# Attention with token mixing on one core: one batch instead of two mixed by seven products, single accumulator banks, and transfers issued by ScalarE

## The chip, the cores and the metric

The kernel runs on one core of one Trainium2 chip. The metric is device microseconds of one execution, from start to end. Three runs of the kernel before were timed; one further execution was recorded by the profiler, and every number of the profile is from that one.

## The reference, cut to what matters

Four batches, eight heads, 768 tokens, head size 64. The attention is masked: a query sees a key only when both fall to the same one of 16 cluster centroids. Its output is the input x (4 x 768 x 512) of a second part, the token mixing, and the change is in that part:

```python
    theta = x @ w_theta
    cos_t, sin_t = (np.cos(theta), np.sin(theta))
    zr = x * cos_t
    zi = x * sin_t
    yr = np.einsum('ts,bsd->btd', w_tok_r, zr)
    yi = np.einsum('ts,bsd->btd', w_tok_i, zi)
    y = yr + yi
    u = x + y
    return (u + np.maximum(u @ w_ch, 0.0)).astype(np.float32)
```

`w_tok_r` and `w_tok_i` are 768 x 768, `w_theta` and `w_ch` 512 x 512. All is float32 to the eye of the caller.

## The kernel before, in words

**The parts.** The attention of all batches runs first and leaves x transposed in device memory (`xT_d`). The mixing then goes batch by batch, b = 0 to 3, and in each batch over six tiles of 128 tokens. The tiles are numbered through, n = 6b + t. Matmuls are taken as three products of high and low parts (`hi`, `lo`; the names with h and l at the end), so each float32 product is three matmuls.

**One tile's angle.** `theta_parts` splits the tile's columns of x (`xs`, one DMA on SP's queue, line 925) into `xh` (a cast on ScalarE, line 935) and `xl`. `rotation_angle` makes theta in one PSUM bank `tp` by 12 matmuls 128x512 (line 659). `rotation_reduce` takes it modulo 2 pi on VectorE (`kk`, `rab`, lines 666 to 668), and ScalarE takes the absolute value (line 670) and sine and cosine (line 985 in plain batches, 964 in the others). `rotation_turn` transposes the tile's own block `xb` into `xn` (VectorE, line 652) and then issues the loads of the next tile's block: `xb` has one buffer, and four DMAs of 64 KB fill it (line 647, on SP's queue). VectorE multiplies sine and cosine by `xn` (lines 987 and 971).

**The plain way of mixing** (`mix`, batches 0 and 1, as `PLAIN = 2` says). Each tile adds into y, one PSUM tile of six banks [128, 6, 512], with 48 matmuls (line 1024), 288 in a batch. Then `channel_plain` comes: `add_y` adds y to x (twelve VectorE instructions, line 1152; casts `uh` on ScalarE, line 1154; low parts `ul` on GpSimd, line 1155), `channel_products` multiplies by `w_ch` in eight groups of 12 matmuls (line 1162; the banks are two single ones `cp` and the six of y), and `channel_out` takes the maximum with zero, adds and writes `ot` (VectorE, line 1169, two buffers), which a DMA on SP's queue carries out (line 1171).

**The way by seven products** (`mix_forms`, batches 2 and 3). The two 768 x 768 weights are cut in quarters and summed into seven "forms" per tile (`W_SUM`, `make_forms`: VectorE sums `sum` line 1061, ScalarE casts 1062, GpSimd low parts 1063, DMAs out to device memory as `wf` 1064; the sources are loaded into `ws` tiles). `load_forms` brings a tile's forms back, seven DMAs on SP's queue. `split_z` makes the matching sums of z (`zt` on VectorE, lines 1087 to 1090; `zf` on ScalarE and GpSimd, 1096 and 1097). Each half of the channels then needs 126 matmuls 128x384 over six tiles (line 1112), 252 in a batch. Product 4 has the bank `four`, the other six have the banks of y. Between the halves, `add_products` adds the seven sums to x (VectorE, line 1121) and frees the banks. The second half of z is kept in device memory (`zd`, stored on line 977, loaded back as `zb` on line 1077). `split_u_part` and `channel` are what `add_y` and `channel_plain` are in the plain way.

**The order.** Attention and plain batches are ordered by a list scheduler with its own model of each engine; it may move instructions far from where the program has them. The part by seven products keeps the order in which it is written (`in_order(begin)`). There, tile n + 2 has its angle while tile n is mixed. The making of the forms is a generator (`new_forms`) that the loop over plain tiles advances, five steps at each tile from n = 1 on:

```python
        mix(b, t)
        if 0 < n < PLAIN * NT - 1:
            for _ in range(5):
                next(new_forms, None)
        if n == PLAIN * NT - 2:
            run(new_forms)
            load_forms(0)
            load_forms(1)
```

**Queues and semaphores.** All DMAs of the mixing are issued by SP in the kernel before. Each DMA, whoever issues it, reports on one of eight completion semaphores taken in turn (`DMAHW0` to `DMAHW7` in the lists below), and waits until the DMA that used the same semaphore before it is done.

Of the kernel before, what the change touches and what calls it, by code (L numbers as in the profile page):

```python
# [9 lines left out]
F32 = mybir.dt.float32  # L10
# [4 lines left out]
ALU = mybir.AluOpType  # L15
AX = mybir.AxisListType
PSUM = bass.MemoryType.PSUM
# [24 lines left out]
def kernel(  # L42
# [595 lines left out]
    def load_blocks(n):  # L638
        if n == B * NT:
            return  # L640
        b, t = divmod(n, NT)
        xb = blocks[n] = ma[0].tile([P, DM], F32, tag="xb", name=f"xb{n}")


        for a in range(P // 32):
            src = xT_d[b][:, :, t * P + 32 * a:t * P + 32 * a + 32]
            nc.sync.dma_start(  # L647
                out=xb[32 * a:32 * a + 32].rearrange("c (n m r) -> c n m r", n=NP, m=P // 32),
                in_=src.rearrange("(m c) n r -> c n m r", c=32))

# [194 lines left out]
    def mpool(name, bufs=1, **kw):  # L845
        return mctx.enter_context(tc.tile_pool(name=name, bufs=bufs, **kw))

    pm = [mpool("pm0", space=PSUM)]
    y = mpool("py", space=PSUM).tile([P, 6, 512], F32, name="y")
    pm.append(mpool("pm1", space=PSUM))  # L850
    mx = mpool("mx")
    ma.append(mpool("ma1"))
# [12 lines left out]
    def mbank(name):  # L865
        banks[0] += 1
        return pm[(banks[0] - 1) % 2].tile([P, 512], F32, tag="bank", name=name)
# [51 lines left out]
    def load_columns(n):  # L919

        b, t = divmod(n, NT)
        if 0 < b < B:
            columns[n] = mxs.tile([P, NCT, P], F32, tag="xs", name=f"xs{n}")
            with tc.issue_after(last_load[0].ins):
                nc.sync.dma_start(out=columns[n], in_=xT_d[b][:, :, t * P:(t + 1) * P])

    PLAIN = 2
    turning = {}

    def theta_parts(n, eng, after=None):  # L930
# [43 lines left out]
    def keep_turned(b, t, rab):  # L974
        zs[b, t] = rab
        z_d[b, t] = dram.tile([P, 2, DM // 2], F32, tag=f"z{t}", name=f"zd{b}_{t}", bufs=2)
        nc.sync.dma_start(out=z_d[b, t], in_=rab[:, :, DM // 2:DM])

    def rotate(b, t, rab, xn):
        if b < PLAIN:  # L980
# [21 lines left out]

    def y_at(d, c0, c1):
        bank, c = divmod(d * S + c0, 512)
        return y[:, bank, c:c + c1 - c0]

    def cuts(d, c0=0, c1=S):

# [55 lines left out]
                nc.sync.dma_start(out=w_f[t][:, m - 1], in_=f(to))  # L1064
                yield

    def load_forms(t):
        for m in ORDER:
            nc.sync.dma_start(out=f(forms[t][m]), in_=w_f[t][:, m - 1])

    second = {}
# [28 lines left out]
    four = {}  # L1100

    def product(m):
        return four[0][:, 0:HS] if m == 4 else y[:, Y_AT[m], 0:HS]

    def mix_forms(tiles, first, last):

# [9 lines left out]
    def add_products(b, h, k):  # L1116

        x = xts[b][:, 2 * h:2 * h + 2].rearrange("p d (l n) -> p (d l) n", l=2)

        def add(to, of, op):  # L1120
            nc.vector.tensor_tensor(out=to, in0=to, in1=of, op=op)  # L1121

        def twice(m):
            return product(m).unsqueeze(1).broadcast_to([P, 2, HS])

        if k == 0:
            add(x[:, 0:3:2], twice(4), ALU.add)
            add(x[:, 1:4:2], twice(3), ALU.subtract)
            add(x[:, 0:4:3], twice(1), ALU.add)
        else:  # L1130
            add(x[:, 0:4:3], y[:, 2:4, 0:HS], ALU.subtract)
            add(x[:, 1:3], y[:, 2:4, 0:HS], ALU.add)
            add(x[:, 3], product(6), ALU.add)
            add(x[:, 0], product(7), ALU.subtract)

    def split_u_part(b, h, us, eng):

# [35 lines left out]
    def channel_plain(b):  # L1173
        us = [add_y(b, ch * HS, (ch + 1) * HS) for ch in range(2)]
        for x in range(2 * NCT):
            ch, e = divmod(x, NCT)
            cp = (mbank(f"cp{b}_{x}") if x < 2 else y[:, x - 2])[:, 0:HS]
            channel_products(cp, e, us[ch], range(NCT))
            channel_out(b, e, ch, cp)

# [19 lines left out]
    for n in range(PLAIN * NT):  # L1200
        b, t = divmod(n, NT)
        theta(*divmod(n + AHEAD, NT))
        if b == 0:
            weights_after[0] = splits[n + 1]
            next(late_weights, None)
        mix(b, t)
        if 0 < n < PLAIN * NT - 1:
            for _ in range(5):
                next(new_forms, None)
        if n == PLAIN * NT - 2:  # L1210
            run(new_forms)
            load_forms(0)
            load_forms(1)
        if t == NT - 1:
            if b == PLAIN - 1:
                load_forms(2)
                load_forms(3)
            channel_plain(b)
            load_x(b + 1)
# [22 lines left out]
        if n in turning:  # L1242
            turned(n)

    load_forms(4)
    before(PLAIN * NT + 2)
    z = split_z(PLAIN, 0, 0)
    for b in range(PLAIN, B):
        for t in range(NT - 1):
            n = b * NT + t  # L1250
            done(n + 1)
            angle(n + 2)
            before(n + 3)
            now, z = z, split_z(b, t + 1, 0)
            mix_forms([(t, now)], t == 0, False)
            if t == 0:
                load_forms(5)
            turn(n + 2)
            if t == NT - 2:
                load_z(b, 5)  # L1260
# [12 lines left out]
        for t in (5, 4, 3, 2, 1, 0):  # L1273
            mix_forms([(t, now)], t == 5, t == 0)
            if t == 5:
                load_forms(0)
            if t > 1:
                now, z = z, split_z(b, t - 2, 1)
                load_z(b, t - 4)
# [10 lines left out]
        if b + 1 < B:  # L1290
            z = split_z(b + 1, 0, 0)
        channel(b, us)
        if b + 1 < B:
            load_x(b + 1)
            load_forms(4)
    in_order(begin)
    mctx.close()

# [50 lines left out]
```

## Time and profile before

| what | value |
|---|---|
| runs | 886.58 us (median of 3; 885.67 to 886.92) |
| the profiled execution | 885.21 us, span from first to last instruction 883.4 us |
| granted TensorE clock over the span | 0.959 |
| busy share of the span | PE 89%, VectorE 72%, GpSimd 64%, ScalarE 47% |
| matmuls | 5316 |

By stages, the profiled execution is: attention to 449.8 us; mixing of batch 0 to 521.7; a stretch without matmuls to 539; channels of batch 0 to 576; batch 1 to 632.3 and its channels to 660.4; batch 2 to 772.8; batch 3 to 883.4.

How to read it: the page of the profile gives busy time by engine. A table by windows gives the same for stretches of time. A timeline row has the start, the duration of one instruction, engine, line, operation, output and input, the shape, how many of them stand in the row, and in brackets how long the engine had been idle and what released it. A row of waits has the engine and line that waited, the engine and line waited for, the sum in us, how often, and the longest.

### The profile page before, as it was taken

What the parts mean: (1) busy time and instruction counts of PE and PEld (TensorE: products, weight loads), DVE (VectorE), ACT (ScalarE), POOL (GpSimd) and SP (SyncE); (2) the same over time, 40 slices, a digit from 0 to 9 for tenths busy, and PEclk for the clock granted to TensorE, in tenths of its full rate; (3) what the DMA queues carried; (4) which work ended last, traced back from release to release, by engine and by line L of the source; (5) the groups of instructions that cost most, each with busy time, mean ns of one, the idle gap of its engine ahead of it and who ended that gap; (6) DMA issues with size and microseconds to landing.
All of it is one profiled execution on the core that took longest, in us unless ns stands there. A gap on an engine that the chain in (4) does not pass through costs nothing. (4 is left out here: it accounts for less than half of the span.)

```text
span 883.4 us, 14497 instructions
## 1 busy us (share of the span) xinstructions
PE 788.0 (89%) x5316; PEld 576.5 (65%) x5316; DVE 640.4 (72%) x789; ACT 415.3 (47%) x835; POOL 563.6 (64%) x345
## 2 busy tenths in 40 slices
PE   9999999999999999988999955899986878886786
PEld 6656666666666666655567844788765767775675
DVE  7689999999999999976957976745534865237552
ACT  3566666766766666654545444433303332023210
POOL 3677899899999998894739668436603433122420
PEclk9999999999999999998999996999997979898989
DMA  3122333342444433362368665889848452194501
GB/s 127 62 72 65 122 124 119 118 140 84 141 154 152 134 123 115 100 216 95 97 180 235 176 186 189 268 300 329 311 174 287 105 182 75 63 347 91 185 12 72
DMA packets 115234, 135.37 MB, mean 153 GB/s; under 512 B 62226, under 2 KB 81308, under 8 KB 114780
## 3 DMA queue, kind: packets, MB, share of 16 engines
q1 hardware_dynamic: 115164, 134.45, 47.9%
q8 instruction: 42, 0.69, 0.3%
q14 instruction: 28, 0.23, 0.1%
HBM read 96.99 MB, written 37.33 MB: 152 GB/s over the span
## 5 line engine op out<-in xcount | busy, mean ns | idle before, releaser
L485 ACT ACTIVATE at<-sc 128x384 f32<-128x384 f32 x384 | 174.0, 493 | 97.9 <-PE sc L409 51.6
L431 DVE TENSOR_REDUCE nm<-m 128x1 f32<-128x768 f32 x192 | 180.3, 947 | 29.8 <-PE m L409 27.8
L496 POOL TENSOR_TENSOR acc<-at,at 128x768 f32<-128x768 f32 x64 | 125.9, 1967 | 40.1 <-ACT at L485 40.1
L409 PE MATMUL m<-hk,hq 64*128 64x384 f32 x384 | 147.6, 385 | 0.2 <-DVE nm L431 0.2
L557 PE MATMUL av<-at,vt 128*64 128x384 f32 x768 | 145.7, 500 | 0.2 <-ACT xt L572 0.2
L496 POOL TENSOR_TENSOR acc<-acc,at 128x768 f32<-128x768 f32 x64 | 132.9, 2076 | 10.8 <-ACT at L485 8.7
L409 PE MATMUL m<-mk,mq 64*128 64x384 f32 x384 | 128.5, 335 | 0.1
L409 PE MATMUL sc<-hq,hk 64*128 64x384 f32 x384 | 117.2, 392 | 6.6 <-ACT at L485 6.4
L409 PEld LDWEIGHTS sc<-hq,hk 64*128 64x128 f32 x384 | 55.4, 184 | 69.2 <-issue 25.3
L409 PE MATMUL sc<-hq,lk 64*128 64x384 f32 x384 | 97.4, 336 | 0.0
L409 PE MATMUL sc<-mq,mk 64*128 64x384 f32 x384 | 97.3, 336 | 0.0
L409 PE MATMUL sc<-lq,hk 64*128 64x384 f32 x384 | 97.0, 335 | 0.0
L557 PEld LDWEIGHTS av<-at,vt 128*64 128x64 f32 x768 | 46.6, 136 | 59.1 <-issue 54.1
L1097 POOL TENSOR_TENSOR zf<-zt,zf 128x384 fp32r<-128x384 f32 x24 | 24.8, 1031 | 82.1 <-ACT zf L1096 82.1
L409 PEld LDWEIGHTS m<-hk,hq 64*128 64x128 f32 x384 | 70.7, 184 | 2.0 <-DVE nm L431 1.4
L409 PEld LDWEIGHTS m<-mk,mq 64*128 64x128 f32 x384 | 71.4, 186 | 0.8 <-DVE mk L374 0.4
L500 DVE TENSOR_TENSOR acc<-acc,acc 128x768 f32<-128x768 f32 x30 | 63.5, 2117 | 0.0
L1063 POOL TENSOR_TENSOR ws<-sum,ws 128x384 fp32r<-128x384 f32 x30 | 35.2, 1178 | 33.2 <-ACT ws L1062 33.2
L409 PEld LDWEIGHTS sc<-mq,mk 64*128 64x128 f32 x384 | 54.6, 185 | 0.0
L409 PEld LDWEIGHTS sc<-lq,hk 64*128 64x128 f32 x384 | 54.5, 186 | 0.0
L409 PEld LDWEIGHTS sc<-hq,lk 64*128 64x128 f32 x384 | 54.4, 185 | 0.0
L1024 PE MATMUL y<-wr_hi,z 128*128 128x512 f32 (+1 forms) x192 | 49.9, 341 | 4.1 <-DVE ot L1169 2.5
(222 smaller groups left out, 1775.2 us busy)
## 6 DMA issues: line engine op xcount, KB each, us to landing
wf<-ws SPq DMA_DIRECT2D x42, 384.0 KB
ws<-wf SPq DMA_DIRECT2D x20, 384.0 KB
vt<-in_v_dram SPq DMA_DIRECT2D x16, 384.0 KB
rb<-sd SPq DMA_DIRECT2D x32, 192.0 KB
xT_d<-xt SPq DMA_DIRECT2D x16, 384.0 KB
xb<-xT_d SPq DMA_DIRECT2D x96, 64.0 KB
out_dram<-ot SPq DMA_DIRECT2D x32, 192.0 KB
rawq<-in_qT_dram SPq DMA_DIRECT2D x15, 384.0 KB
```

Of the source, the lines that this page charges most:

```text
L409: nc.tensor.matmul(out, lhsT=stat[r, cols], rhs=mov[r, over], start=start, stop=stop)
L431: nc.vector.tensor_reduce(out=s["nm", a][:, j, i // 2:i // 2 + 1], in_=s["m", j][:, :, 0:HS], op=ALU.max, axis=AX.XY, negate=True)
L485: last_exp[0] = nc.scalar.activation(out=s["at", a, i][:, j], in_=s["sc", j], func=AF.Exp, scale=SCALE)
L496: last_acc[0] = nc.gpsimd.tensor_tensor(out=s["acc", a, x], in0=prev, in1=at, op=ALU.add)
L500: nc.vector.tensor_tensor(out=s["acc", a, 0], in0=s["acc", a, 0], in1=s["acc", a, 1], op=ALU.add)
L557: nc.tensor.matmul(s["av"][64 * j:64 * j + 64], lhsT=s["vt"][:, i, j, :], rhs=s["at", a, i][:, j], start=(i == 0), stop=(i == NT - 1))
L1024: last_mix[0] = nc.tensor.matmul(y_at(d, c0, c1), lhsT=zz[:, d * P:(d + 1) * P], rhs=ww[:, c0:c1], start=first and lead, stop=last, skip_g ...
L1063: nc.gpsimd.tensor_tensor(out=lo, in0=src, in1=f(hi), op=ALU.subtract)
L1097: nc.gpsimd.tensor_tensor(out=l_, in0=of, in1=f(h_), op=ALU.subtract)
```

## The change: what it does

- `PLAIN` goes from 2 to 3: batches 0, 1 and 2 are mixed in the plain way and only batch 3 by seven products.
- The forms are made six steps at a tile, from n = 6 on, so in the program's text in batches 1 and 2.
- y is six PSUM tiles of one bank each, and the additions of the second half of the channels (`add_products`) go by single products: six instructions instead of four.
- `load_forms` is issued in two pieces for each tile, at other places; the x of batch 3 is loaded earlier only if a batch by products came before it, which is no longer the case.
- The loads of `xb` (for n of 2 and more) and `xs` and the stores of `zd` go from SP's queue to ScalarE's: 88 + 18 + 6 = 112 DMAs.

The diff, cut:

```diff
-            nc.sync.dma_start(
+            (nc.sync if n < 2 else nc.scalar).dma_start(
                 out=xb[32 * a:32 * a + 32].rearrange("c (n m r) -> c n m r", n=NP, m=P // 32),
...
-    y = mpool("py", space=PSUM).tile([P, 6, 512], F32, name="y")
+    py = mpool("py", space=PSUM)
+    y = [py.tile([P, 512], F32, name=f"y{x}") for x in range(6)]
...
-                nc.sync.dma_start(out=columns[n], in_=xT_d[b][:, :, t * P:(t + 1) * P])
-
-    PLAIN = 2
+                nc.scalar.dma_start(out=columns[n], in_=xT_d[b][:, :, t * P:(t + 1) * P])
+
+    PLAIN = 3
...
-        nc.sync.dma_start(out=z_d[b, t], in_=rab[:, :, DM // 2:DM])
+        nc.scalar.dma_start(out=z_d[b, t], in_=rab[:, :, DM // 2:DM])
...
-    def load_forms(t):
-        for m in ORDER:
+    def load_forms(t, ms=ORDER):
+        for m in ms:
...
-            add(x[:, 0:4:3], y[:, 2:4, 0:HS], ALU.subtract)
-            add(x[:, 1:3], y[:, 2:4, 0:HS], ALU.add)
-            add(x[:, 3], product(6), ALU.add)
-            add(x[:, 0], product(7), ALU.subtract)
+            for m, less, more in ((5, 0, 1), (2, 3, 2), (6, None, 3), (7, 0, None)):
+                if less is not None:
+                    add(x[:, less], product(m), ALU.subtract)
+                if more is not None:
+                    add(x[:, more], product(m), ALU.add)
...
-        if 0 < n < PLAIN * NT - 1:
-            for _ in range(5):
+        if NT <= n < PLAIN * NT - 1 and t < NT - 1:
+            for _ in range(5 if b == 0 else 6):
                 next(new_forms, None)
...
-    load_forms(4)
...
-            if t == 0:
-                load_forms(5)
+            if t < 4:
+                load_forms(*((4, ORDER[:4]), (4, ORDER[4:]), (5, ORDER[:4]), (5, ORDER[4:]))[t])
+            if t == 2 and b > PLAIN:
+                load_x(b)
...
             if t == 5:
-                load_forms(0)
+                load_forms(0, ORDER[:4])
+            if t == 4:
+                load_forms(0, ORDER[4:])
...
         channel(b, us)
-        if b + 1 < B:
-            load_x(b + 1)
-            load_forms(4)
```

Three places show how the rows of the engines move. In the lists, `[waits ...]` names the engines or completion semaphores that a row waits for.

TensorE, the beginning of the channels of batch 1. Before, `cp` are the two single banks, `uh_0` and `uh_384` the casts of the two halves of tokens, and y is one tile:

```order
L1162 MATMUL cp_0_7703<-uh_0_7671,wch_hi 128x384 [waits Activation_49]
L1162 MATMUL cp_1_7719<-uh_0_7671,wch_hi 128x384 [waits DVE_49]
L1162 MATMUL cp_0_7703<-uh_0_7671,wch_hi 128x384 [waits Activation_49]
L1162 MATMUL cp_1_7719<-uh_0_7671,wch_hi 128x384
L1162 MATMUL cp_0_7703<-uh_0_7671,wch_hi 128x384 [waits Activation_49]
L1162 MATMUL cp_1_7719<-uh_0_7671,wch_hi 128x384
L1162 MATMUL cp_0_7703<-uh_0_7671,wch_hi 128x384 [waits Activation_49]
L1162 MATMUL cp_0_7703<-uh_0_7671,wch_lo 128x384 x4
```

The same place of the changed kernel, where y is the tiles `y_6054` to `y_6059`:

```order
L1164 MATMUL cp_0_7610<-uh_0_7578,wch_hi 128x384 [waits Activation_49]
L1164 MATMUL cp_1_7626<-uh_0_7578,wch_hi 128x384 [waits DVE_49]
L1164 MATMUL y_6054<-uh_0_7578,wch_hi 128x384 [waits DVE_49]
L1164 MATMUL y_6055<-uh_0_7578,wch_hi 128x384 [waits DVE_49]
L1164 MATMUL y_6056<-uh_384_7594,wch_hi 128x384 [waits DVE_49,Activation_49]
L1164 MATMUL cp_0_7610<-uh_0_7578,wch_hi 128x384 [waits Activation_49]
L1164 MATMUL cp_1_7626<-uh_0_7578,wch_hi 128x384
L1164 MATMUL y_6054<-uh_0_7578,wch_hi 128x384
```

The scheduler now opens five groups on five banks with the first cast of u, where it had two; each bank of y waits for its own additions only.

ScalarE, one tile of a batch by products: `rab_2` are the angles of tile 2, `xs` and `xh_4` the columns of tile 4, `zf_2_0` the sums of z of tile 2. Before:

```order
L670 ACTIVATE rab_2_8273<-rab_2_8273 128x512 [waits DVE_49,Pool_49]
L964 ACTIVATE rab_2_8273<-rab_2_8273 128x512 [waits Activation_49]
L964 ACTIVATE rab_2_8273<-rab_2_8273,halfpi 128x512
L935 CAST xh_4_8713<-xs_8635 128x512 [waits DMAHW5_49,PE_49]
L1096 CAST zf_2_0_8719<-zt_2_0_8720 128x384 [waits DVE_49,PE_49]
L1096 CAST zf_2_0_8719<-rab_2_8273 128x512 [waits DVE_49]
```

The same place after:

```order
L670 ACTIVATE rab_2_8529<-rab_2_8529 128x512 [waits DMAHW2_49,DVE_49,Pool_49]
L647 DMA xb_8606<-xT_d_63 32x16x32 [waits DMAHW7_49,DMAHW4_49,DVE_49]
L647 DMA xb_8606<-xT_d_63 32x16x32 [waits DMAHW1_49]
L647 DMA xb_8606<-xT_d_63 32x16x32 [waits DMAHW3_49]
L647 DMA xb_8606<-xT_d_63 32x16x32 [waits DMAHW5_49]
L965 ACTIVATE rab_2_8529<-rab_2_8529 128x512 [waits Activation_49]
L965 ACTIVATE rab_2_8529<-rab_2_8529,halfpi 128x512
L978 DMA zd_2_8615<-rab_2_8529 256x1x256 [waits DMAHW0_49,DVE_49]
L926 DMA xs_8630<-xT_d_63 128x4x128 [waits DMAHW1_49,Pool_49]
L936 CAST xh_4_8633<-xs_8558 128x512 [waits DMAHW6_49,PE_49]
L1097 CAST zf_2_0_8639<-zt_2_0_8640 128x384 [waits DVE_49,PE_49]
L1097 CAST zf_2_0_8639<-rab_2_8529 128x512 [waits DVE_49]
```

Four issues now stand between the absolute value and the sine of the same tile, and two more ahead of the cast of a later one.

VectorE, the change from the first half of the channels to the second in a batch by products (`zb_4` and `zt_4_1`: the second half of z of tile 4). Before:

```order
L1121 TENSOR_TENSOR xT_7825<-xT_7825,y 128x2x384 [waits DVE_49]
L1087 TENSOR_TENSOR zt_4_1_8257<-zb_4_8202 128x256 [waits DMAHW2_49,Pool_49]
L1088 TENSOR_TENSOR zt_4_1_8257<-zb_4_8202 128x128
L1090 TENSOR_TENSOR zb_4_8202<-zb_4_8202 128x256 [waits DVE_49]
L1121 TENSOR_TENSOR xT_7825<-xT_7825,y 128x2x384
L1121 TENSOR_TENSOR xT_7825<-xT_7825,y 128x768
L1121 TENSOR_TENSOR xT_7825<-xT_7825,y 128x384 [waits DVE_49]
L1121 TENSOR_TENSOR xT_7825<-xT_7825,y 128x384
```

The same place after:

```order
L1122 TENSOR_TENSOR xT_8520<-xT_8520,y_6055 128x2x384 [waits DVE_49,PE_49]
L1088 TENSOR_TENSOR zt_4_1_8885<-zb_4_8847 128x256 [waits DMAHW6_49,Pool_49]
L1089 TENSOR_TENSOR zt_4_1_8885<-zb_4_8847 128x128
L1091 TENSOR_TENSOR zb_4_8847<-zb_4_8847 128x256 [waits DVE_49]
L1122 TENSOR_TENSOR xT_8520<-xT_8520,y_6056 128x384 [waits PE_49]
L1122 TENSOR_TENSOR xT_8520<-xT_8520,y_6056 128x384
L1122 TENSOR_TENSOR xT_8520<-xT_8520,y_6057 128x384 [waits PE_49]
L1122 TENSOR_TENSOR xT_8520<-xT_8520,y_6057 128x384
L1122 TENSOR_TENSOR xT_8520<-xT_8520,y_6058 128x384 [waits DVE_49,PE_49]
L1122 TENSOR_TENSOR xT_8520<-xT_8520,y_6059 128x384 [waits PE_49]
```

Each addition waits for its own product's matmuls now, and the sums of z still stand between the third addition and the fourth.

More of the change, by code (lines that the diff above doesn't have):

```diff
@@ L1004, in y_at @@
         bank, c = divmod(d * S + c0, 512)
-        return y[:, bank, c:c + c1 - c0]
+        return y[bank][:, c:c + c1 - c0]
     def cuts(d, c0=0, c1=S):
@@ L1102, in product @@
     def product(m):
-        return four[0][:, 0:HS] if m == 4 else y[:, Y_AT[m], 0:HS]
+        return four[0][:, 0:HS] if m == 4 else y[Y_AT[m]][:, 0:HS]
     def mix_forms(tiles, first, last):
@@ L1176, in channel_plain @@
             ch, e = divmod(x, NCT)
-            cp = (mbank(f"cp{b}_{x}") if x < 2 else y[:, x - 2])[:, 0:HS]
+            cp = (mbank(f"cp{b}_{x}") if x < 2 else y[x - 2])[:, 0:HS]
             channel_products(cp, e, us[ch], range(NCT))
```

## The prediction

> **What bounds the kernel now.** I read the table by windows first, cut where a batch or its channels begin, because the shares of the whole span are two thirds attention, which the change leaves alone. Columns: from and to, the length, then busy time and number of instructions of each engine, the granted clock, the DMA share and rate.
>
> ```profile
> core 0: us, PE busy (x) PEld busy (x) DVE busy (x) ACT busy (x) POOL busy (x), PEclk, DMA share, GB/s
> 449.80:521.70 71.90, 69.50 (x368) 57.41 (x360) 57.88 (x71) 32.79 (x57) 48.21 (x32) 1.00 0.69 201
> 521.70:539.00 17.30, 0.00 (x0) 0.00 (x0) 12.00 (x17) 8.99 (x17) 11.20 (x9) 0.65 0.64 202
> 539.00:576.00 37.00, 31.46 (x144) 27.35 (x144) 24.57 (x43) 15.36 (x30) 22.48 (x22) 0.93 0.75 242
> 576.00:632.30 56.30, 56.22 (x312) 48.54 (x312) 26.41 (x34) 19.81 (x36) 29.31 (x25) 1.00 0.93 310
> 632.30:660.40 28.10, 22.08 (x112) 19.06 (x112) 11.49 (x27) 3.96 (x8) 7.81 (x8) 1.00 0.61 215
> 660.40:772.80 112.40, 85.71 (x405) 77.36 (x406) 62.15 (x90) 30.09 (x53) 37.92 (x31) 0.88 0.48 146
> 772.80:851.30 78.50, 61.52 (x302) 56.26 (x301) 41.17 (x68) 21.39 (x38) 27.27 (x24) 0.91 0.56 179
> 851.30:883.40 32.10, 20.88 (x98) 18.67 (x96) 10.94 (x16) 1.56 (x2) 0.00 (x0) 0.87 0.13 50
> ```
>
> Plain mixing (fourth row) is bound by TensorE: 56.22 of 56.30 us busy at full clock. Batches by seven products (the last three rows) are not: TensorE has 85.71 of 112.40 us there, at a clock of 0.88, and the first of them alone takes twice a plain mixing. So next come TensorE's waits, in five windows: 539 to 576, 633 to 661, 661 to 773, 773 to 851.5 and the end (sum in us, times, longest):
>
> ```profile
> PE cp L1162 <- ACT uh L1154: 17.7, 2, 17.4
> PE y L1024 <- DVE ot L1169: 2.5, 1, 2.5
> PE y L1162 <- DVE ot L1169: 2.4, 3, 1.0
> ...
> PE y L1162 <- DVE ot L1169: 3.0, 4, 0.9
> PE cp L1162 <- ACT uh L1154: 1.7, 1, 1.7
> PE tp L659 <- DVE ot L1169: 0.8, 1, 0.8
> ...
> PE tp L659 <- ACT xh L935: 8.6, 1, 8.6
> ...
> PE tp L659 <- DVE rab L667: 5.9, 1, 5.9
> PE y L1112 <- DVE xT L1121: 3.5, 1, 3.5
> PE tp L659 <- ACT xh L935: 3.4, 1, 3.4
> ...
> PE y L1162 <- DVE xT L1121: 3.8, 1, 3.8
> PE y L1162 <- DVE ot L1169: 3.3, 5, 0.7
> ```
>
> Three kinds show: the start of the channels waits for the sums of y (17.4 us in batch 0, 1.7 in batch 1), channels wait for `ot` though another bank is free, and by seven products the chain over the angles, VectorE and ScalarE comes late.
>
> **Batch 2, plain instead of by products.** Its price is made of three rates:
>
> ```profile
> 576.05:609.81 33.76, 33.76 (x192) 29.36 (x192) 1.00 0.98 318
> 609.81 1.08 PE L659 MATMUL tp<-wth_hi,xh 128*128 128x512 f32 x4
> 612.55 0.51 PE L1024 MATMUL y<-wr_hi,z 128*128 128x512 f32 x2
> 756.72 0.51 PE L1162 MATMUL four<-u,wch_hi 128*128 128x384 f32 x2
> 757.76 0.51 PE L1162 MATMUL y<-u,wch_hi 128*128 128x384 f32 x2
> ```
>
> The first row is the table for line 1024 alone: 192 matmuls in 33.76 us, so 288 take 50.6. An angle lasts from 609.81 to 612.55, 2.74 us, and six take 16.4. From 756.72 to 757.76 six channel matmuls pass, 0.173 us each, and 96 take 16.6. With 2.5 us of waiting between mixing and channels (batch 1 had 1.7; a bank more to follow) and 1 us elsewhere, batch 2 takes 87.1 us instead of 112.4: **-25.3**. By matmuls alone the seven products are the cheaper way (252 x 0.173 = 43.7 against 50.6); what goes is their waits and their slow clock. As tile 14 no longer has its angle at the end of batch 1 (the window there has 112 matmuls, 16 beyond the 96), 2.74 + 3 x 0.173 = **-3.3** there; and for the longer gap ahead of batch 1's channels **+0.8**, for odd waits in its mixing **+1**.
>
> **The gap ahead of batch 0's channels.** VectorE's rows there, and one of batch 1:
>
> ```profile
> 530.00 0.56 DVE L1061 TENSOR_TENSOR sum<-ws,ws 128x384 f32<-128x384 f32 x1 [2.61 <-DMA ws<-wd2r]
> 534.48 1.29 DVE L987 TENSOR_TENSOR rab<-rab,xn 128x512 f32<-128x512 f32 x2 [0.98 <-ACT rab L985]
> 535.80 0.71 DVE L652 STREAM_TRANSPOSE xn<-xb 128x512 f32<-128x512 f32 x1
> 537.92 0.87 DVE L1152 TENSOR_TENSOR xT<-y,xT 128x384 f32<-128x384 f32 x2
> 632.79 4.05 DVE L1152 TENSOR_TENSOR xT<-y,xT 128x384 f32<-128x384 f32 x12
> ```
>
> TensorE is done at 521.7, and the first addition comes at 537.92: VectorE is behind with sums of the forms and with angles. In batch 1 all twelve additions take 4.05 us at once. With the sums begun later, ten instead of fourteen stand ahead of the first addition (4 x 0.56 plus a longer one of 1.33, some 3.6 us less), the load that is waited for 2.61 us is early, and with a wait for each bank the additions may begin before the last tile is done, the next tile's product and transposition (1.29 + 0.71 and their 0.98 of idle) behind them. 17.4 less 3.6, 2.6 and 3 would be 8; I take 9: **-8.4**, between 17.4 (nothing gained) and 1.7 (as batch 1). The sums aren't gone, they move to batches 1 and 2, where VectorE has 26.41 busy of 56.30 us; if that cover failed, R4 below is the price.
>
> **Single banks in the channels of batches 0 and 1.** A group that needs one bank no longer waits for the last `ot` that reads another: of 2.5 + 2.4 + 3.0 + 0.8 = 8.7 us I leave 1.0: **-7.7** (ends: 0, if two `ot` buffers bind and not the banks; 8.7).
>
> **ScalarE's queue.** 112 issues leave SP. What stands around one in a batch by products:
>
> ```profile
> 686.80 0.68 DVE L666 TENSOR_SCALAR kk<-tp 128x512 int32<-128x512 f32 x1
> 690.74 2.63 SPq L647 DMA_DIRECT2D xb<-xT_d  x4
> 690.84 0.63 ACT L964 ACTIVATE rab<-rab 128x512 f32<-128x512 f32 x1
> 691.50 1.31 DVE L971 TENSOR_TENSOR rab<-rab,xn 128x512 f32<-128x512 f32 x2 [0.79 <-ACT rab L964]
> 694.76 0.68 DVE L666 TENSOR_SCALAR kk<-tp 128x512 int32<-128x512 f32 x1
> 696.20 1.28 POOL L1097 TENSOR_TENSOR zf<-rab,zf 128x512 fp32r<-128x512 f32 x1
> ```
>
> SP's four issues begin 0.1 us before the first sine and take 2.63 us. Now they stand on ScalarE ahead of that sine, VectorE's product already waits 0.79 us for it, and behind the product stand the sums of z and the next tile's `kk`. No issue by ScalarE is in the trace: it costs between 0 and SP's 0.66, and a gain is open only if SP's queue were late, for which no row of batch 3 speaks. I take 0.63, so a tile goes from 7.96 us (`kk` to `kk`) to 10.5. In plain batches a tile has five such issues, 3.2 us, beside 11.1 us of matmuls (48 x 0.176 + 2.74); ScalarE has 19.81 busy of 56.30 us there, so I cost them at nothing. The one place without cover is the start:
>
> ```profile
> 445.03 0.71 DVE L652 STREAM_TRANSPOSE xn<-xb 128x512 f32<-128x512 f32 x1 [4.50 <-DMA xb<-xT_d]
> ```
>
> The loads of tile 2 wait for this transposition, which waits for the loads of tile 1, and the attention's last exponentials now queue behind the first of them on ScalarE: **+2.5** (0 to 6).
>
> **Batch 3** then comes out so: the first angle 2.8; three tiles with loads 3 x 10.5 = 31.5; one without, 8.0; from its next `kk` to the end of the low parts (694.76 to 697.48) 2.6; its 21 matmuls 3.6; the change of halves 3 (the wait of 3.5 is shortened little, as sums of z still stand between the additions); six tiles of 21 x 0.173 = 3.64, 21.8; waits for GpSimd 0.5; channels 17.6 (96 x 0.173 and 1 us: the additions by product remove most of the 3.8 and the banks most of the 3.3); the tail of 4.1 as before. Together 95.5 against 78.5 + 32.1 = 110.6: **-15.1**. The 5.9 and 3.4 us at its start go, because the angles of tiles 18 and 19 are made in plain batch 2. Loading the forms in pieces costs nothing as long as tiles of 10.5 us cover it.
>
> **The sum:** 2.5 - 8.4 - 7.7 - 3.3 + 0.8 + 1 - 25.3 - 15.1 = -55.5, against the profiled execution's 885.2: 829.7; its median stands 1.4 higher. I say **830**.
>
> **The rivals.**
>
> R1, ScalarE's issues are hidden: the tile of batch 3 stays at 7.96, 7.5 us less: 822. For it, ScalarE is busy 21.39 of 78.50 us; against it, the sine is what VectorE waits for. Chance 0.15.
>
> R2, loads late in batch 3. `xs` and `xb` share the engines with the forms; before, in that batch, the angle waited 3.4 us for `xh` and in the batch ahead 8.6. If both return, with 3 us of slower clock, 15 us more: 845. For it, the form loads sit at the same tiles; against it, DMA is busy only 0.56 there. Chance 0.12. The Trainium skill ("DMA: Bandwidth & Descriptors", section "Issuing engines are not separate DMA queues") says that DMAs started by ScalarE, SyncE or GpSimd end on the same 16 engines and interleave, and that another issuer saves sequencer time alone; by that rule ScalarE's queue buys no bandwidth, and 845 stands against 830.
>
> R3, single banks release nothing: the 7.7 stay, and 3.3 + 3.8 of batch 3's channels and a little of its change of halves: 19 more, 849. Against it, the waits are for `ot` of any bank while y is one tile. Chance 0.08.
>
> R4, batches 1 and 2 come to look like batch 0, because the sums of the forms now fall on them: gaps of 17 instead of 2.5 twice, and the first gap less by half of what I took: some 37 more, 867. Chance 0.10.
>
> R5, the other side: ScalarE's queue is in order, and its loads take turns with SP's bulk transfers on eight completion semaphores, so that casts and sines stand behind an unfinished bulk DMA:
>
> ```profile
> ACT ws L1062 <- DMA wf<-ws: 14.2, 10, 5.5
> ```
>
> That is ScalarE's wait for DMAs in batch 1 before: ten times, 5.5 us at most. To eat the 55.5 us, each of 17 plain tiles would have to take 3.3 us over its 11.1. ScalarE needs about 7.2 us a tile with the issues, so it would have to stand 7.2 us in each, five times the mean of that row (1.4): 887 and more. Chance 0.04. R6, the whole does nothing measurable: 0.01.
>
> **How the numbers follow.** My own case has 0.50, with 816 to 843 as its range: the gap of batch 0 from 1.7 to 17.4 (-7, +8), the start (-2.5, +3.5), the channels (-1, +7.7), the tile of batch 3 (-7.5, 0), taken half at a time. The range over all, 808 to 856, holds R1, R2 and R3 and leaves out R4 to R6 (0.15) and a little below. Faster by over 0.2% (about what a measurement of this kernel can tell from none) is everything but R5 and R6: 0.95.
>
> **What would show it.** The windows: batch 2 at about 87 us with its channels, batch 3 at 95. Among TensorE's waits, those for `ot` gone from the channels, and about 9 us for batch 0's `uh`. In VectorE's rows, the first additions of y before the last matmul of the mixing, and `kk` to `kk` in batch 3 at 10.5 (right) or 8 (R1). ScalarE waiting for DMAs by tens of us in batches 1 and 2 would be R5; gaps of 17 us there, R4. The forecast fails if a plain batch 2 is not bound by TensorE.

## The result and the profile after

The changed kernel takes 826.49 us (median of 3; 825.71 to 827.44) against 886.58: a ratio of 0.9325 (95% interval 0.9304 to 0.9346), 60.1 us less. The forecast was 830, in a range of 808 to 856. The profiled execution has a span of 825.5 us at a mean clock of 0.981.

The table by windows of the changed kernel, cut at its own stages: mixing of batch 0, the stretch without matmuls, channels of batch 0 with the mixing of batch 1, channels of batch 1, all of batch 2, then batch 3 in two rows.

```profile
core 0: us, PE busy (x) PEld busy (x) DVE busy (x) ACT busy (x) POOL busy (x), PEclk, DMA share, GB/s
451.86:524.45 72.59, 68.50 (x360) 57.41 (x360) 65.43 (x71) 34.94 (x61) 50.50 (x33) 1.00 0.63 183
524.45:534.19 9.74, 0.00 (x1) 0.00 (x1) 8.20 (x14) 4.75 (x10) 6.98 (x5) 0.60 0.65 188
534.19:621.39 87.20, 87.00 (x456) 76.36 (x457) 52.79 (x80) 35.75 (x68) 54.54 (x47) 0.97 0.67 214
621.39:641.75 20.36, 17.85 (x97) 16.46 (x96) 7.11 (x17) 6.66 (x14) 12.13 (x12) 1.00 0.61 195
641.75:726.23 84.48, 84.12 (x457) 74.13 (x457) 39.77 (x64) 25.22 (x44) 26.88 (x22) 1.00 0.66 199
726.23:805.22 78.99, 62.23 (x301) 55.98 (x301) 41.17 (x72) 20.37 (x36) 25.87 (x22) 0.94 0.54 169
805.22:825.50 20.28, 16.80 (x97) 16.48 (x96) 9.17 (x16) 1.57 (x2) 0.00 (x0) 1.00 0.21 78
```

Batch 2 is bound by TensorE now: 84.12 of 84.48 us busy, at full clock. Batch 3 is not: 62.23 of 78.99. TensorE's waits over the whole mixing:

```profile
PE cp L1164 <- ACT uh L1156: 9.7, 1, 9.7
PE tp L659 <- DVE rab L667: 8.1, 2, 5.5
PE four L1113 <- POOL zf L1098: 3.7, 4, 1.2
PE y L1025 <- ACT z L991: 3.3, 2, 2.8
PE y L1113 <- DVE ot L1171: 2.8, 1, 2.8
PE y L1164 <- ACT uh L1156: 2.5, 2, 1.3
...
PE y L1113 <- DVE xT L1122: 0.5, 1, 0.5
```

No channel matmul waits for `ot` any more, and the change of halves in batch 3 waits 0.5 us instead of 3.5.

### The profile page after: what moved, and what is told of

Read it like the earlier page. It is cut to its first block, busy times and chain, and to the rows that moved or that the text cites. A ratio compares the mean times of both kernels' runs of the same rounds, so it can differ in the third digit from the quotient of the medians.

```text
span 825.5 us, 14427 instructions
## 1 busy us (share of the span) xinstructions
PE 778.0 (94%) x5352; PEld 568.7 (69%) x5352; DVE 617.5 (75%) x757; ACT 410.5 (50%) x827; POOL 554.7 (67%) x335
## 5 line engine op out<-in xcount | busy, mean ns | idle before, releaser
L993 POOL TENSOR_TENSOR z<-rab,z 128x512 fp32r<-128x512 f32 x36 | 49.8, 1403 | 57.8 <-ACT z L991 55.6
L1025 PE MATMUL y<-wr_hi,z 128*128 128x256 f32 (+1 forms) x288 | 76.1, 339 | 4.3 <-ACT z L991 3.3
L1025 PE MATMUL y<-wi_hi,z 128*128 128x512 f32 (+1 forms) x288 | 75.1, 339 | 0.3 <-POOL z L993 0.2
L1025 PEld LDWEIGHTS y<-wr_hi,z 128*128 128x128 f32 x288 | 49.8, 188 | 12.9 <-ACT z L991 4.4
L1025 PEld LDWEIGHTS y<-wi_hi,z 128*128 128x128 f32 x288 | 49.5, 188 | 7.7 <-POOL z L993 1.3
```

The source lines that it names most:

```text
L993: nc.gpsimd.tensor_tensor(out=zl, in0=tr, in1=f(zh), op=ALU.subtract)
L1025: last_mix[0] = nc.tensor.matmul(y_at(d, c0, c1), lhsT=zz[:, d * P:(d + 1) * P], rhs=ww[:, c0:c1], start=first and lead, stop=last, skip_g ...
```

## The experiments

Each experiment was timed beside the kernel before on the same chip, and its ratio is to that; the medians of the kernel before lay between 884.2 and 885.8 us there, and at 886.58 beside the change itself.

| kernel | median us | ratio to before, 95% interval |
|---|---|---|
| the change | 826.49 | 0.9325 (0.9304 to 0.9346) |
| the change, all DMAs on SP | 819.26 | 0.9263 (0.9231 to 0.9295) |
| the change, `xb` of the last three tiles on SP | 814.16 | 0.9208 (0.9173 to 0.9243) |
| the change, `xb` behind the sines | 820.47 | 0.9275 (0.9249 to 0.9302) |
| the change, y as one tile | 857.83 | 0.9697 (0.9666 to 0.9729) |
| the change, forms made early | 829.91 | 0.9386 (0.9357 to 0.9415) |
| before, three plain batches | 859.13 | 0.9714 (0.9679 to 0.9749) |
| before, single banks | 856.05 | 0.9670 (0.9629 to 0.9711) |
| before, both | 828.01 | 0.9379 (0.9346 to 0.9412) |
| before, ScalarE's queue | 885.95 | 1.0018 (1.0001 to 1.0035) |
| four plain batches | 797.76 | 0.9016 (0.8987 to 0.9045) |
| the same, `xb` of tile 2 on SP | 798.44 | 0.9028 (0.8989 to 0.9066) |
| the same, all DMAs on SP | 785.03 | 0.8878 (0.8856 to 0.8899) |

**ScalarE's queue, undone.**

```diff
-            (nc.sync if n < 2 else nc.scalar).dma_start(
+            nc.sync.dma_start(
...
-                nc.scalar.dma_start(out=columns[n], in_=xT_d[b][:, :, t * P:(t + 1) * P])
+                nc.sync.dma_start(out=columns[n], in_=xT_d[b][:, :, t * P:(t + 1) * P])
...
-        nc.scalar.dma_start(out=z_d[b, t], in_=rab[:, :, DM // 2:DM])
+        nc.sync.dma_start(out=z_d[b, t], in_=rab[:, :, DM // 2:DM])
```

> The changed kernel with every load and store back on SP's queue; the other parts stay. My theory: ScalarE's issues are paid for in the last batch (three tiles at some 10.5 us or more instead of 8, and one sine that stood 8.1 us behind four loads) and at the start (1.65 us); in the plain batches, where TensorE is busy without a break, the queue does nothing. Then the kernel is 5 to 10 us faster than the changed one, 817 to 821. Rival: SP's queue holds the loads of the tiles back behind its own form loads and output stores, as the 8.6 us wait for xh before showed, so the move paid: 830 to 840.

819.26 us: as my theory had it in sum, but not in its parts. Windows from the first matmul of the mixing to the first product of batch 3, and from there to the end, first of the changed kernel, then with all on SP:

```profile
451.86:728.99 277.13, 260.24 (x1380) 226.62 (x1381) 173.30 (x242) 107.32 (x194) 151.03 (x118) 0.98 0.65 200
728.99:825.50 96.51, 76.27 (x385) 70.21 (x383) 50.34 (x88) 21.94 (x38) 25.87 (x22) 0.95 0.46 146
```

```profile
449.99:733.71 283.72, 262.83 (x1384) 229.61 (x1381) 169.91 (x244) 107.01 (x194) 146.81 (x117) 0.96 0.65 199
733.71:815.70 81.99, 72.86 (x385) 67.94 (x383) 51.35 (x88) 22.05 (x38) 25.56 (x22) 0.98 0.56 175
```

ScalarE's queue costs 14.5 us in batch 3 and 1.9 at the start, and gives 6.6 in the plain batches, where I had said that it does nothing. (The two profiled executions are 9.8 us apart and the medians 7.2, so each part is good to some 2 us.) The 6.6 are themselves a sum. With all on SP, batch 0 takes 2.8 us less from its first mixing matmul to its first channel matmul (79.49 against 82.33), and the stretch from there to the end of batch 1 takes 9.4 more (116.98 against 107.56). In that stretch TensorE waits 2.8 us for additions of y in the channels of batch 0, and 2.4 and 4.0 us for `uh` in those of batch 1, where the change has 1.2 and 1.3 us.

What in SP's queue brings these waits is not shown. The waits of SP's queue in the mixing, with all on SP, show the stores of the forms, which wait for GpSimd with the tiles' loads queued behind them:

```profile
SPq L1065 <- POOL ws L1064: 49.8, 26, 7.0
```

In the change these stores wait no less (64.0 us from 534 to 650, against 35.6 in that stretch with all on SP), but the tiles' loads are on the other queue. VectorE's waits from 534 to 650 us, with all on SP, show a transposition that stands 8.2 us for its block; below it is SP's row for the loads of that block:

```profile
DVE xn L652 <- DMA xb<-xT_d: 8.2, 1, 8.2
```

```profile
571.08 6.69 SPq L647 DMA_DIRECT2D xb<-xT_d  x4
```

That block was not behind a store: its four issues begin as soon as the transposition before it is done (571.05) and take 6.69 us instead of 2.6. And TensorE, which has other work, shows no wait between this place and the end of the mixing of batch 1.

**Where in batch 3 the queue costs.** First, SP issues the blocks of tiles 21 to 23 alone:

```diff
-            (nc.sync if n < 2 else nc.scalar).dma_start(
+            (nc.sync if n < 2 or n > 20 else nc.scalar).dma_start(
```

> The changed kernel with the four loads of each block of the last three tiles issued by SP; xs and zd stay on ScalarE, and all plain batches too. My theory: in the last batch the loads' place on ScalarE, ahead of the sines, is what costs (three times 2.6 us, and 5.5 us more where the first four stood behind form loads), while in the plain batches the queue saves some 6 us: 811 to 817, below the kernel with all on SP (819). Rival: the blocks are late whoever issues them, because the forms are being loaded: 822 to 827.

Second, ScalarE goes on issuing them, but behind the sines:

```diff
-            theta_turn(n)
-            sines(turning[n][4])
+            xh, xl, xn, kk, rab, tp = turning[n]
+            rotation_reduce(n, tp, kk, rab)
+            nc.vector.transpose(out=xn, in_=blocks.pop(n))
+            sines(rab)
+            load_blocks(n + 1)
```

> The changed kernel with the four loads of a block issued by ScalarE behind the sine and cosine of the last batch instead of ahead of them. My theory: it is the place in ScalarE's order that costs, not who issues: nearly all of the 12 us that issuing by SP gave comes back here too, 814 to 818. Rival: ScalarE stands behind the loads all the same, with zd, xs and the casts queued behind them, among them the first loads that wait for form loads: 820 to 825.

814.16 and 820.47: moving the issue to SP gives 12.3 us, moving it behind the sines gives 6.0, half of it. From the first product of batch 3 to the end the two take 83.71 and 89.73 us (385 matmuls each), against 96.51. ScalarE's rows at the first of the three tiles, first of the changed kernel, then with the loads behind the sines:

```profile
733.13 0.63 ACT L670 ACTIVATE rab<-rab 128x512 f32<-128x512 f32 x1 [19.87 <-issue]
733.70 8.14 ACTq L647 DMA_DIRECT2D xb<-xT_d  x4
741.89 0.63 ACT L965 ACTIVATE rab<-rab 128x512 f32<-128x512 f32 x1 [8.12 <-DMA xb<-xT_d]
```

```profile
733.79 5.58 ACTq L647 DMA_DIRECT2D xb<-xT_d  x4
741.81 0.59 ACTq L978 DMA_DIRECT2D zd<-rab  x1
...
743.19 0.62 ACT L936 CAST xh<-xs 128x512 fp32r<-128x512 f32 x1 [9.73 <-DVE rab L668]
```

Four issues take 2.65 us where nothing holds them (SP had 2.63); here they took 8.14. By the listing in the part on the change, each of the four waits for an earlier DMA on its completion semaphore, and what SP issued just ahead are, beside output stores, form loads of 384 KB each:

```profile
731.40 2.31 SPq L1070 DMA_DIRECT2D ws<-wf  x4
733.80 0.57 SPq L1070 DMA_DIRECT2D wr_hi<-wf  x1
```

That it was these that held the four is inferred from the order of issues and semaphores; no run took the form loads alone away. Behind the sines the stall no longer holds the sines, but it still holds `zd`, `xs` and the cast of a later tile. So both theories were half right: the place counts, and the queue counts. With SP as the issuer the blocks are late too (the transpositions wait 3.66, 1.79 and 0.54 us for them), yet nothing but the blocks is. The Trainium skill ("DMA: Bandwidth & Descriptors", section "Issuing engines are not separate DMA queues") says that all issuers share the same 16 engines and another issuer saves sequencer time alone; the traces are in line with it, in that the second tile's transposition waited 3.66 us with SP's queue and 3.25 with ScalarE's, but no run here tests it.

**Single banks, undone.**

```diff
-    py = mpool("py", space=PSUM)
-    y = [py.tile([P, 512], F32, name=f"y{x}") for x in range(6)]
+    y6 = mpool("py", space=PSUM).tile([P, 6, 512], F32, name="y")
+    y = [y6[:, x] for x in range(6)]
```

> The changed kernel with y as one tile of six banks; the other parts stay. My theory: the channels of three plain batches wait for ot again (8.7 us in two before, so some 13 in three), the first additions can't begin before the whole mixing is done (1.7 us in batch 1 and 2 each, 3 in batch 0), and the last batch gets its 3.5 us wait between the halves and 3.8 + 3.3 in its channels back: 18 to 28 us slower than the changed kernel, 844 to 854. Rival: the two ot buffers and their stores bind, not the banks: within 5 us of the changed kernel, 826 to 832.

857.83: 31 us slower than the change, over the upper end of my theory. TensorE's waits:

```profile
PE cp L1164 <- ACT uh L1156: 19.5, 3, 15.9
PE y L1164 <- DVE ot L1171: 13.5, 15, 3.3
```

The waits for `ot` come out as worked out (13); the gap of batch 0 is 15.9 us again, though the forms are made late. So it was the banks, not the sums of the forms, that shortened it. VectorE's rows show how, first of this kernel, then of the change:

```profile
538.77 4.06 DVE L1154 TENSOR_TENSOR xT<-y,xT 128x384 f32<-128x384 f32 x12
```

```profile
531.77 0.74 DVE L1154 TENSOR_TENSOR xT<-y,xT 128x384 f32<-128x384 f32 x2
```

With one tile all twelve additions stand together, behind the next tile's product and transposition and four sums; with single banks the first two come ahead of all of these, though still 7.3 us after the last matmul of the mixing.

**The making of the forms, moved back.**

```diff
-        if NT <= n < PLAIN * NT - 1 and t < NT - 1:
-            for _ in range(5 if b == 0 else 6):
+        if 0 < n < PLAIN * NT - 1:
+            for _ in range(5):
```

> The changed kernel with the forms made from the second tile of batch 0 on, five steps at a tile, as before; the other parts stay. My theory: the sums stand ahead of the first additions of batch 0 again and its gap goes from 9.7 back to 13 to 17 us, with nothing gained elsewhere, as batches 1 and 2 have no gap to lose: 830 to 834. Rival: the gap shrank by the additions for single banks alone: 826 to 828.

829.91, some 3 us slower, and by another way than I said: the gap of batch 0 is 7.3 us, smaller than the 9.7 of the change, and batches 1 and 2 take longer (200.6 instead of 194.8 us from the first channel matmul to the first product), with a gap of 3.76 us ahead of the channels of batch 1. My theory of that gap is refuted.

**One part alone, on the kernel before.** Three plain batches:

```diff
-    PLAIN = 2
+    PLAIN = 3
```

> The kernel before with three plain batches instead of two, and nothing else. My theory: the third batch costs 87 us and some 8 of waits for ot and for the sums of y that one tile of six banks brings, against 112.4 by products: 17 to 25 us faster than before, 861 to 869. Rival: the waits of a batch by products only move into the last one, which starts cold: within 8 us of before, 878 to 887.

859.13: 26 us, a little over my theory. The gap of batch 0 is 17.4 us there, as before, and waits for `ot` are 13.0 us. Single banks, with the additions as in the change:

```diff
-    y = mpool("py", space=PSUM).tile([P, 6, 512], F32, name="y")
+    py = mpool("py", space=PSUM)
+    y = [py.tile([P, 512], F32, name=f"y{x}") for x in range(6)]
...
-            add(x[:, 0:4:3], y[:, 2:4, 0:HS], ALU.subtract)
...
+            for m, less, more in ((5, 0, 1), (2, 3, 2), (6, None, 3), (7, 0, None)):
...
```

> The kernel before with y as six tiles of one bank and the additions by single products, and nothing else. My theory: the waits for ot in two plain channels (8.7), those in two channels by products (3.8 + 3.3 each), the change of halves (3.5 and 2.9 in part) and a few us of the gap of batch 0 go: 20 to 30 us faster than before, 856 to 866. Rival: what single banks save in the channels comes back as a wait of the next batch for its angles, whose chain by products is late anyway: 8 to 14 us faster, 872 to 878.

856.05: 29 us. The gap of batch 0 falls to 10.5 by the banks alone; a new wait stands beside what they save (9.7 us of TensorE for form loads), and the sum is as my theory had it. Both edits together:

> The kernel before with three plain batches and y as six tiles of one bank with additions by single products; forms made as early and loaded as whole as before, and all on SP's queue. Alone the two gave 26 and 29 us. With the later making of the forms and their loading in pieces the same stands at 819. My theory: the two help each other (a plain batch with single banks has no gaps, some 10 us that neither gives alone), and the forms' time and pieces add 3 to 5 us: 820 to 825. Rival: the two only add up (55), and the forms' time and pieces bring the rest: 828 to 833.

828.01: the rival was right, the two add up (56 us). This kernel is within 1.5 us of the whole change. The change with all on SP has the later making of the forms and their loading in pieces besides, and is 8.8 us faster (819.26). From the first product of batch 3 to the end this kernel takes 94.9 us where that one takes 82.0; from the channels of batch 0 to those of batch 1 it takes 89.4 us where that one takes 93.8. The 13 us in batch 3 are probably the pieces, which I had costed at nothing: SP issues seven form loads in a row (732.35 to 736.63) ahead of the first block's loads here, three or four between two blocks there, and the longest wait of a transposition for its block is 4.76 us here, 1.22 there:

```profile
749.72 0.71 DVE L652 STREAM_TRANSPOSE xn<-xb 128x512 f32<-128x512 f32 x1 [4.76 <-DMA xb<-xT_d]
```

ScalarE's queue:

```diff
-            nc.sync.dma_start(
+            (nc.sync if n < 2 else nc.scalar).dma_start(
                 out=xb[32 * a:32 * a + 32].rearrange("c (n m r) -> c n m r", n=NP, m=P // 32),
...
-                nc.sync.dma_start(out=columns[n], in_=xT_d[b][:, :, t * P:(t + 1) * P])
+                nc.scalar.dma_start(out=columns[n], in_=xT_d[b][:, :, t * P:(t + 1) * P])
...
-        nc.sync.dma_start(out=z_d[b, t], in_=rab[:, :, DM // 2:DM])
+        nc.scalar.dma_start(out=z_d[b, t], in_=rab[:, :, DM // 2:DM])
```

> The kernel before with xb, xs and zd on ScalarE's queue, and nothing else. My theory: two batches by products now have the four loads ahead of the sines (some 2.6 us in seven tiles, 18 us, and stalls behind form loads), and two plain batches gain a few us: slower than before by 8 to 20 us, 893 to 906. Rival: before, these batches wait for xs and xh that come late by SP (8.6 and 3.4 us), and the move takes these waits away: 872 to 884.

885.95, no change, and neither theory had it. Windows before and with the move, from the first mixing matmul to the end of batch 1, batch 2, and batch 3:

```profile
450.21:660.40 210.19, 178.86 (x932) 152.36 (x928) 131.94 (x189) 80.92 (x147) 119.01 (x94) 0.96 0.75 239
660.40:775.62 115.22, 88.53 (x417) 79.69 (x418) 63.57 (x94) 31.13 (x55) 38.69 (x32) 0.88 0.48 146
775.62:883.40 107.78, 79.58 (x385) 72.61 (x383) 50.69 (x80) 21.92 (x38) 26.50 (x24) 0.90 0.43 141
```

```profile
453.61:668.50 214.89, 180.89 (x927) 155.02 (x927) 138.96 (x193) 84.57 (x154) 125.79 (x99) 0.94 0.74 234
668.50:774.08 105.58, 84.47 (x418) 76.22 (x418) 54.58 (x89) 27.33 (x48) 33.18 (x28) 0.95 0.49 149
774.08:883.80 109.72, 80.74 (x385) 74.05 (x383) 48.57 (x80) 21.83 (x38) 26.92 (x24) 0.87 0.41 136
```

The start costs 3.4 us, the plain batches 4.7, batch 3 1.9, and batch 2 gains 9.6. There are two opposite effects, and each of my two theories had one of them only.

**No products at all.** `PLAIN = 4`, and everything of the forms left out:

```diff
-    PLAIN = 3
+    PLAIN = 4
...
-    late_weights, new_forms = late(), make_forms()
+    late_weights = late()
...
-        if NT <= n < PLAIN * NT - 1 and t < NT - 1:
...
-                load_forms(3)
             channel_plain(b)
-            load_x(b + 1)
-    us = [u_tile(f"u{x}") for x in range(4)]
...
-    in_order(begin)
+            if b + 1 < B:
+                load_x(b + 1)
```

> The changed kernel with all four batches plain, and no forms made or loaded. It computes the same. My theory: seven products cost more than they save here since their chain over the angles leaves TensorE idle; batch 3 then takes 50.6 of mixing, four angles at 2.74, 16.6 of channels, some 1.5 of waits and the tail of 4, 83.8 us instead of 99.3, and the gap of batch 0 shrinks by the sums that are gone (0 to 5 us): 805 to 812. Rival: with its angles made early the last batch by products is near its matmuls (43.7 against 50.6), so without it the kernel is slower by up to 7 us: 827 to 834.

797.76, 7 us under the lower end of my range and 29 under the change: batch 3 takes 81.7 us to the end of the span where batch 2 takes 83.6, and the gap of batch 0 falls to 3.6. Two more of this kind. With the start's load on SP:

```diff
-            (nc.sync if n < 2 else nc.scalar).dma_start(
+            (nc.sync if n < 3 else nc.scalar).dma_start(
```

> All four batches plain, no forms, and the loads of tile 2 issued by SP instead of ScalarE. It computes the same. My theory: the last exponential of the attention no longer stands 1.9 us behind a load that waits for a transposition: 2 us less than with all from tile 2 on by ScalarE (797.8), 794 to 797. Rival: the start is set by VectorE's copy of the attention's output: 797 to 799.

And with all loads on SP (`zd` is gone with the products):

```diff
-            (nc.sync if n < 2 else nc.scalar).dma_start(
+            nc.sync.dma_start(
...
-                nc.scalar.dma_start(out=columns[n], in_=xT_d[b][:, :, t * P:(t + 1) * P])
+                nc.sync.dma_start(out=columns[n], in_=xT_d[b][:, :, t * P:(t + 1) * P])
```

> All four batches plain, no forms, and all loads and stores on SP's queue. It computes the same. My theory: in the plain batches ScalarE's queue pays only because SP's queue carries the making of the forms, whose stores stood 36 us waiting for GpSimd, with one block's transposition waiting 8.2 us for its load in batch 1; without forms SP's queue is free, and the time is that of the kernel with ScalarE's queue: 794 to 800. Rival: SP's queue holds the loads back for other reasons (output stores that wait for ot), and the 6.6 us are lost here too: 803 to 808.

798.44: the mixing starts 2.9 us earlier (451.19 instead of 454.08), as said, but the gap of batch 0 is 6.4 instead of 3.6, and the time is the same; the start alone is worth nothing while VectorE is behind in batch 0. 785.03 for all on SP, below both theories: the best kernel of the study, 41 us under the change. Its two windows, batch 0's mixing and all the rest to the last matmul, and those of four plain batches with ScalarE's queue:

```profile
450.93:517.93 67.00, 67.00 (x365) 57.67 (x362) 52.73 (x76) 34.26 (x57) 36.80 (x25) 1.00 0.54 137
517.93:780.07 262.14, 262.14 (x1441) 234.58 (x1439) 103.87 (x183) 71.18 (x126) 74.69 (x65) 1.00 0.25 67
```

```profile
454.08:524.81 70.73, 67.17 (x360) 57.55 (x360) 54.03 (x68) 32.08 (x52) 40.18 (x24) 1.00 0.42 106
524.81:790.83 266.02, 265.01 (x1440) 236.79 (x1440) 108.50 (x189) 73.62 (x130) 75.69 (x66) 0.99 0.25 67
```

With all on SP, TensorE is busy in all of the 329.14 us from the first matmul of the mixing to the last; there is no gap left, not even batch 0's. ScalarE's queue costs 3.2 us at the start and 7.6 behind it, though it does the same loads. So the 6.6 us that it gave in the change's plain batches do not come without the forms. That SP's part in making the forms is the cause is not shown, and one run speaks against it: in the kernel before, SP carries the making of the forms through batches 0 and 1 too, and there the same move cost 4.7 us.

## Why the prediction came out right, point by point

The measured sum, stage by stage, against the profiled execution before (57.9 us of span):

- **Start, +2.5: right in place and near in size.** The last exponential waited for the transposition, as said, and the mixing starts 1.65 us later (450.21 to 451.86). Over all kernels here it starts between 451.86 and 454.08 us in the seven with this load on ScalarE, and between 449.85 and 451.19 in the seven with it on SP. ScalarE's rows of the change:

```profile
445.39 0.64 ACTq L647 DMA_DIRECT2D xb<-xT_d  x1
446.08 0.49 ACT L485 ACTIVATE at<-sc 128x384 f32<-128x384 f32 x1 [1.83 <-DVE xn L652]
```

- **Mixing of batch 0: no term, measured +1.1** (71.46 to 72.59).
- **Gap of batch 0, -8.4: measured -7.65 (17.39 to 9.74), right in size by luck, wrong in cause.** I gave 6.2 us to sums and a load that come later, and 3 to the banks. (In the rows before, the sums between the last matmul and the first addition are four, of 3.0 us together, not 3.6.) By the runs it is the banks: 10.5 with them alone, 15.9 without them, 7.3 with the sums early. The sign that I had named, additions of y before the last matmul of the mixing, shows in batches 1 and 2 but not in batch 0.
- **Channels and gaps of batches 0 and 1, -7.7, -3.3, +0.8 and +1, together -9.2: measured -13.8** (94.87 to 87.20 us from the first channel matmul of batch 0 to that of batch 1, and 26.47 to 20.36 behind it). I let the gap ahead of the channels grow; it vanished. VectorE's first addition of batch 1 starts at 619.30, while TensorE still mixes, up to 621.39:

```profile
619.30 0.74 DVE L1154 TENSOR_TENSOR xT<-y,xT 128x384 f32<-128x384 f32 x2
...
621.04 0.51 PE L1025 MATMUL y<-wi_hi,z 128*128 128x256 f32 x2
621.39 0.51 PE L1164 MATMUL cp<-uh,wch_hi 128*128 128x384 f32 x2
```

- **Batch 2, -25.3: measured -28.0** (112.46 to 84.48). The three rates were right, 50.6 + 16.4 + 16.6 = 83.6; the 3.5 us of waits that I added were not there.
- **Batch 3, -15.1: measured -11.3** (110.54 to 99.27). In the terms of the sum: the first `kk` came 4.6 us after the first angle matmul instead of 2.8, as VectorE stood 5.13 us for an output store; the three tiles with loads took 35.2 instead of 31.5; from there to the second half it was 14.6 instead of 14.2; the change of halves, the six tiles and their waits took 24.6 instead of 25.3; channels and tail 20.3 instead of 21.7. What failed is the tile's period of 10.5: from `kk` to `kk` it was 14.0, 12.7 and 8.6.

```profile
730.86 0.68 DVE L666 TENSOR_SCALAR kk<-tp 128x512 int32<-128x512 f32 x1
...
744.84 0.69 DVE L666 TENSOR_SCALAR kk<-tp 128x512 int32<-128x512 f32 x1
...
751.10 0.71 DVE L652 STREAM_TRANSPOSE xn<-xb 128x512 f32<-128x512 f32 x1 [3.25 <-DMA xs<-xT_d]
...
757.50 0.69 DVE L666 TENSOR_SCALAR kk<-tp 128x512 int32<-128x512 f32 x1
...
763.79 1.31 DVE L972 TENSOR_TENSOR rab<-rab,xn 128x512 f32<-128x512 f32 x2 [3.39 <-ACT rab L965]
...
766.09 0.68 DVE L666 TENSOR_SCALAR kk<-tp 128x512 int32<-128x512 f32 x1
```

  The place was the one named, the four issues ahead of the sine. But I had costed an issue at 0.63 us and left the wait for its completion semaphore to R5 alone, as a matter of whole batches; it struck here once, for 5.5 us, and the late blocks of R2 struck behind it. In the third tile nothing held the issues. There VectorE's product waited 3.39 us for the sine instead of 0.79, the 2.6 us that I had named; but two VectorE instructions were shorter than in the kernel before (0.78 instead of 1.80 us on line 668, 0.43 instead of 1.38 on the first sum of z), so that even there the period was not 10.5.

So the forecast was within 3.5 us of the median, and in part by luck. Against the forecast, the stages were off by -0.9 (start), +1.1 (mixing of batch 0), +0.8 (its gap), -4.6 (channels and gaps), -2.7 (batch 2) and +3.8 us (batch 3), which cancel to -2.4. By the parts of the change the errors are larger, and cancel too. Single banks are worth about 30 us (29 alone on the kernel before, 31 taken out of the change), where R3 priced them at 19, without the 3 us that I had given them in the gap. The forms' later making and loading in pieces are worth some 9, where I had 6.2 for the time of making and nothing for the pieces. And ScalarE's queue costs about 7 net, where I had 2.5 + 7.5 of cost and no gain.

Of the rivals, R1 was wrong, since moving the issues away from the sines gave 6 to 12 us; R3 and R4 were wrong (R4's price, by its own terms, is 33 us and not 37); R2 and R5 held in small. The sign that I had named for R5, ScalarE waiting for DMAs by tens of us in batches 1 and 2, did come (29.9 us for stores of the forms), but it cost little there: TensorE was busy in 191.73 of the 194.80 us from the first channel matmul of batch 0 to the first product. What was not tried: the change with form loads whole, and forms made late without pieces, so that the 13 us rest on two kernels that differ in the time of making as well.

## What to carry to other kernels

An accumulator that spans several banks as one tile ties each bank's next use to the last reader of all of them: look for matmuls that wait for an evacuation of another bank, and count what the tile costs at both ends, the first reader's too. A faster algorithm by matmul count (252 x 0.173 against 288 x 0.176 us) is no gain if the work that feeds it leaves TensorE idle; compare it with the plain way at the plain way's full use. And before DMAs move to a computing engine's queue, look at what stands behind them there, and at what they wait for to be issued, not only at how long an issue takes.

## What the runs showed that I had not expected

Four issues by ScalarE take what SP's take, 2.65 us, where nothing holds them. Where, by the order of issues, they met bulk transfers on the completion semaphores they were to use, four took 8.14. SP's issues are held at places too: four took 6.69 us with all on SP.

The same VectorE instruction on 128x512 (line 668) took 1.80 us before and 0.69 in the first tile of the changed batch 3. The long one (second row) starts while GpSimd runs a subtraction, the short one has no GpSimd row beside it:

```profile
688.25 1.29 POOL L1097 TENSOR_TENSOR zf<-rab,zf 128x512 fp32r<-128x512 f32 x1
688.30 1.80 DVE L668 SCALAR_TENSOR_TENSOR rab<-kk,rab 128x512 f32<-128x512 int32 x1
...
732.36 0.69 DVE L668 SCALAR_TENSOR_TENSOR rab<-kk,rab 128x512 f32<-128x512 int32 x1
```

The long one took 1.11 us over the 0.69; GpSimd's row ends at 689.54, 1.24 us in. The Trainium skill ("SBUF — State Buffer", section "SBUF: two separate sides") says that VectorE instructions with two SBUF inputs and GpSimd instructions share one pair of ports, held for a whole instruction while the other waits; these rows agree with it. No run here took GpSimd's work away to show it as the cause.
